# Attention scores issued as one phase of four row strips, long TensorE operations in pieces, and a new order of all queues

## The chip, the cores and the metric

The program runs on one core of a Trainium2 chip. The metric is the time of one execution in microseconds (us) of device time; lower is better. Several executions are timed and their median is given. One more execution is recorded by the hardware profiler; its page and its trace are what is quoted here. The core has five engines, each with a queue of its own that it works off in order: TensorE (PE in the profile, with the loads of its weights as PEld), ScalarE (ACT), VectorE (DVE), GpSimd (POOL) and SyncE (SP), which here only issues transfers. TensorE writes its results to PSUM, which has eight banks of 512 fp32 values in each of 128 partitions.

## The reference

Two kinds of layer alternate, A, B, A, B, on x of 2048 tokens by 512 features, with 32 heads of 16 features each. Cut to what matters:

```python
x = x + A(layernorm(x)); x = x + B(layernorm(x)); x = x + A(layernorm(x)); x = x + B(layernorm(x))

def A(x):                       # 4 segments of 512 tokens, one after the other
    q, k, v = x @ wq, x @ wk, x @ wv
    for s in range(4):
        p = softmax(qs @ ks.T * 0.25 + causal_mask)
        a_dot = p @ vs
        a_mem = (phi(qs) @ M) / (phi(qs) @ z + 1e-6)
        o_s = g * a_mem + (1 - g) * a_dot
        M += phi(ks).T @ vs; z += phi(ks).sum()
    return o @ wo

def B(x):                       # linear attention over all 2048 tokens
    q, k, v = split(x @ wqkv)
    phi(t) = concat(softmax(t @ w_phi), softmax(-(t @ w_phi)))
    kv, z = phi(k).T @ v, phi(k).sum()
    return ((phi(q) @ kv) / (phi(q) @ z + 1e-6)) @ wo
```

Here `phi` of A is `where(t > 0, t + 1, exp(t))`, and `g` is a gate for each head. Input and output are bfloat16.

## The kernel before

`Kernel.build` (line 1363) first only describes the work. Each call of `pe`, `act`, `dve`, `pool`, `either`, `copy` or `dma` makes one operation (`Program.add`, line 305), which has a number, an engine or a choice of engines, and what it reads and writes. An operation of TensorE is a list of matmuls, and it gives one signal when its last matmul is done. Nothing is issued in the order in which it is described. Four tables at the head of the file, made beforehand, settle that: `ORDER` lists the operations' numbers in one order from which every engine's queue follows; `ENGINE` has a letter for each operation that has a choice of engines (a, d, p, s for ScalarE, VectorE, GpSimd, SyncE), in the order in which these operations are made; `SLOTS` gives the buffer that each tile gets, in the order in which tiles are first used; and `AFTER` has pairs (x, y) in which operation x also waits for y. `Program.replay` (line 353) reads the tables, and `finalize` (line 411) derives the semaphore waits from reads, writes and the buffers' former holders, and writes the queues. A negative number in `ORDER` is an idle operation: so many matmuls of 240 columns on zeros (line 1431) whose result nobody reads.

For each of the two A layers and each of its four segments, `a_proj` (line 890) makes queries, keys and values of four tiles of 128 tokens. `a_att` (line 1034) makes the attention. Its work is cut into 18 units for a segment by `stages` (line 1013), 144 in all. A unit fills four PSUM banks, that is two bank pairs of 128 x 1024 scores. A head has only 16 features, so keys are laid out such that four heads stand in four strips of 32 partitions each; a score matmul uses one strip (32 rows of the array) and writes one bank. Strips 0 and 1 write the first pair, strips 2 and 3 the second. Each pair is then read by one exponential on ScalarE (line 1104) into a tile `PT`; on the diagonal, masks follow on VectorE or GpSimd (lines 1110 and 1113); and the p·v matmuls of 17 columns (16 features and the sum) multiply `PT` with `VT`. A bank pair (tile kind `st`) is (0, 1), (2, 3) or (4, 5); banks 4 to 7 also serve all other TensorE results (kinds `gen` and `pv`).

Before the change the loop at line 1078 makes two score operations for a unit, one for each bank pair, each followed by its exponential and masks. If two halves stand next to each other in `ORDER`, the second is written with 10000 added. Then `replay` makes it the first one's `mate`, joins their waits, and `finalize` issues the matmuls of the two in turn, two by two. There are 67 such pairs; the other 77 units are issued as two halves at two places of the queue.

The layers B are made by `b_keys` (line 1190: exponentials `Ek`, sums `Zk`, scaled values `Vt`, then the sum kv over tiles), `b_queries` (line 1265: exponentials of the queries, their sums `bq.sum` and the factor `rho`) and `b_out` (line 1317). B's keys and queries of a segment are worked on during the following attention. `a_out` and `b_last` project the result (`WA_o`, `WB_o`) and add it to `X` by `close` (line 1173), by VectorE or by one more matmul with the identity. `steps` (line 864) cuts a list of matmuls into operations of n matmuls; the projections use it already.

## Time and profile before

| what | us |
|---|---|
| median of 3 runs | 478.32 |
| lowest and highest | 478.20, 478.62 |
| span of the profiled execution, first to last instruction | 476.9 |
| TensorE busy | 465.2 |
| ScalarE busy | 429.7 |
| VectorE busy | 424.0 |
| GpSimd busy | 268.9 |

The profile gives the profiled execution by its span alone; the median of the runs is 1.4 us above it. The costliest groups of instructions show the attention: the exponentials, the masks, the p·v matmuls and the scores (line 520 is the helper that issues every matmul). Columns: line, engine, operation, output and inputs, count; busy us and mean ns of one; idle us of the engine before them, and what ended it.

```profile
L1104 ACT ACTIVATE PT<-PS 128x1024 bf16<-128x1024 f32 x288 | 284.6, 1083 | 7.8 <-PE PS L520 7.5
L1113 POOL TENSOR_SCALAR_AFFINE_SELECT PT<-PT 128x512 bf16<-128x512 bf16 x128 | 83.9, 664 | 30.8 <-DVE D L1110 27.4
L520 PE MATMUL PS<-VT,PT 128*128 128x17 bf16 x2048 | 82.4, 171 | 0.7 <-POOL PT L1113 0.2
L520 PE MATMUL PS<-QT,K 32*128 32x64 bf16 (+2 forms) x2176 | 77.9, 213 | 0.3
```

A group's busy time counts overlapping instructions once, and the ends of matmuls are modelled. How long a TensorE operation really holds the engine is therefore read from the start of its first matmul to the start of the next operation's first one.

### The profile page before, as it was taken

To read this page: it belongs to the slowest core of one execution; us is meant where nothing else is said; L and a number is where in the kernel's file an instruction comes from. 1 tells how busy PE (TensorE), PEld (TensorE's weight loads), DVE (VectorE), ACT (ScalarE), POOL (GpSimd) and SP (SyncE) were. 2 spreads that over 40 slices of the span, in tenths; PEclk is the share of its full clock that TensorE was granted. 3 is DMA by queue.
4 is the path that set the end of the run, shared out by engine and by line. 5 is a ranking of instruction groups with operands and counts; after the bars stand their busy time and mean duration, and the time that the engine had idled before them with its cause. 6 is when DMAs were issued, how large, how long until landed. Compare 5 with 4: busy or idle time off the path is not lost.

```text
span 476.9 us, 19206 instructions
## 1 busy us (share of the span) xinstructions
PE 465.2 (98%) x8309; PEld 319.3 (67%) x8309; DVE 424.0 (89%) x1008; ACT 429.7 (90%) x666; POOL 268.9 (56%) x435
## 2 busy tenths in 40 slices
PE   7999999999999999999999999999999999999997
PEld 6786677567756567557687666766765666665763
DVE  6999899989998988688999999999998888978885
ACT  3989999999999999986799899989999999999742
POOL 3686758656756685510267575784677578761100
DMA  8679661342422132320346417155434121313366
GB/s 264 115 202 147 144 92 25 69 69 47 48 46 47 25 65 51 36 55 4 67 62 97 74 21 134 25 75 83 59 63 63 25 47 33 51 38 58 70 128 186
DMA packets 115091, 35.86 MB, mean 75 GB/s; under 512 B 106816, under 2 KB 115008, under 8 KB 115008
## 3 DMA queue, kind: packets, MB, share of 16 engines
q1 hardware_dynamic: 112608, 32.54, 38.3%
q10 hardware_dynamic: 2400, 2.11, 1.4%
q8 instruction: 65, 1.06, 0.9%
q14 instruction: 18, 0.15, 0.1%
HBM read 6.32 MB, written 2.10 MB: 18 GB/s over the span
## 4 chain that ended last, share of the span: by engine, by line
PE 59%; DVE 18%; ACT 17%; DMA 3%; POOL 2%; issue 1%; POOLq 0%; DVEq 0%
PE PS L520 57%; ACT PT L1104 12%; DVE D L1110 2%; DVE stats L801 2%; DVE Vt L1228 2%; ACT Ek L1200 2%; DVE xn L817 1%; PE PS L601 1%; DMA EQ<-xn 1%; PE PS L1431 1%; DMA OT<-O 1%; DVE O L1139 1%; ACT K L1285 1%; DVE X L1165 1%; DVE Zk L1209 1%
## 5 line engine op out<-in xcount | busy, mean ns | idle before, releaser
L1104 ACT ACTIVATE PT<-PS 128x1024 bf16<-128x1024 f32 x288 | 284.6, 1083 | 7.8 <-PE PS L520 7.5
L1110 POOL TENSOR_TENSOR D<-PT,modd 128x256 bf16<-128x256 bf16 x133 | 91.6, 699 | 54.2 <-ACT PT L1104 39.1
L1113 POOL TENSOR_SCALAR_AFFINE_SELECT PT<-PT 128x512 bf16<-128x512 bf16 x128 | 83.9, 664 | 30.8 <-DVE D L1110 27.4
L520 PEld LDWEIGHTS PS<-VT,PT 128*128 128x128 bf16 x2048 | 75.0, 96 | 19.2 <-POOL PT L1113 2.5
L520 PE MATMUL PS<-VT,PT 128*128 128x17 bf16 x2048 | 82.4, 171 | 0.7 <-POOL PT L1113 0.2
L520 PE MATMUL PS<-QT,K 32*128 32x64 bf16 (+2 forms) x2176 | 77.9, 213 | 0.3
L520 PE MATMUL PS<-VT,D 128*128 128x17 bf16 x512 | 59.9, 170 | 0.0
L520 PEld LDWEIGHTS PS<-QT,K 32*128 32x128 bf16 x2176 | 41.5, 93 | 20.6 <-ACT PT L1104 10.5
L1110 DVE TENSOR_TENSOR D<-PT,modd 128x256 bf16<-128x256 bf16 x123 | 42.9, 362 | 2.9 <-ACT PT L1104 1.5
L520 PEld LDWEIGHTS PS<-VT,D 128*128 128x128 bf16 x512 | 43.2, 96 | 0.0
L1228 DVE TENSOR_TENSOR Vt<-PS,Zk 128x1024 bf16<-128x1024 f32 (+1 forms) x34 | 39.0, 1158 | 2.0 <-PE PS L520 1.0
L801 DVE BATCH_NORM_STATS2 stats<-X 128x6 f32<-128x512 bf16 x56 | 37.3, 681 | 2.5 <-DMA X<-in_A_x_dram 2.2
L1200 ACT ACTIVATE Ek<-PS 128x512 bf16<-128x512 f32 x64 | 37.6, 664 | 0.9 <-PE PS L520 0.9
L520 PE MATMUL PS<-WA_v,xA 128*128 128x256 bf16 x256 | 36.6, 273 | 0.1
L520 PE MATMUL PS<-WA_k,xA 128*128 128x256 bf16 x256 | 36.3, 273 | 0.2 <-POOL xA L907 0.2
L520 PE MATMUL PS<-xA,WA_q 128*128 128x128 bf16 x512 | 35.7, 219 | 0.5 <-DVE MS L986 0.2
L1165 DVE TENSOR_TENSOR X<-X,PS 128x512 bf16<-128x512 bf16 x50 | 33.7, 679 | 2.2 <-PE PS L520 1.8
L1207 POOL TENSOR_TENSOR Vt<-Ek 128x512 f32<-128x512 bf16 x24 | 27.9, 1164 | 12.9 <-ACT Ek L1200 10.4
L520 PEld LDWEIGHTS PS<-xA,WA_q 128*128 128x128 bf16 x512 | 29.8, 98 | 4.6 <-issue 0.6
L520 PE MATMUL PS<-WA_o,OT 128*128 128x512 bf16 x128 | 32.0, 380 | 0.6 <-DMA OT<-O 0.4
L520 PE MATMUL PS<-WB_o,OT 128*128 128x512 bf16 x128 | 32.1, 379 | 0.1
L1304 POOL COPY O<-rho 128x512 bf16<-128x512 bf16 x24 | 14.9, 634 | 26.5 <-DVE rho L1297 23.3
(157 smaller groups left out, 980.7 us busy)
## 6 DMA issues: line engine op xcount, KB each, us to landing
X<-in_A_x_dram SPq DMA_DIRECT2D x3, 512.0 KB, 9.9
EQ<-in_B_wqkv_dram SPq DMA_DIRECT2D x2, 512.0 KB, 5.4
out_dram<-X SPq DMA_DIRECT2D x8, 128.0 KB, 2.0
out_dram<-X ACTq DMA_DIRECT2D x8, 128.0 KB, 1.9
OT<-O SPq DMA_TRANSPOSE x42, 3.2
WB_v<-in_B_wqkv_dram SPq DMA_DIRECT2D x1, 512.0 KB, 4.3
WA_o<-in_A_wo_dram SPq DMA_DIRECT2D x1, 512.0 KB, 6.5
WB_o<-in_B_wo_dram SPq DMA_DIRECT2D x1, 512.0 KB, 4.7
```

What stands on the lines that cost most here:

```text
L520: return e.matmul(o, l, r, start=st, stop=sp, tile_position=(basep(l), basep(o)))
L601: ins = e.transpose(self.bank(gen).bitcast(BF16)[:, dt * 128:(dt + 1) * 128], src()[:, dt * 128:(dt + 1) * 128], self.ident[:])
L801: self.dve(lambda e, t=t, src=src: e.bn_stats(self.stats[:, t, :], src()), 0.603, [held() if held else R("X", t)], [R("stats", t)], name=" ...
L817: self.dve(lambda e, t=t, n=n, xn=xn: e.tensor_scalar(xn.ap[:, n], self.X[:, t, :], self.mv[:, t, 0:1], self.rstd[:, t:t + 1], op0=ALU.sub ...
L1104: self.act(lambda e, st=st, pt=pt: e.activation(pt.ap[:].rearrange("p b c -> p (b c)"), self.ps[:, st.slot[0] * 512:st.slot[0] * 512 + 102 ...
L1110: self.either(lambda e, d=d, k=k, pt=pt: e.tensor_tensor(d.ap[:, :, k, :].rearrange("p b (z c) -> p b z c", z=2), self.ends(pt.ap[:, :, 25 ...
L1113: self.pool(lambda e, q=quarters: e.affine_select(q(), q(), [[0, 4], [1, 128]], ALU.is_ge, 0.0, base=0, channel_multiplier=-1), 0.6, [pt() ...
L1165: self.dve(lambda e: e.tensor_tensor(X[:, t, :], X[:, t, :], self.bank(gen), ALU.add), 0.6, [R("X", t), gen()], [R("X", t)], name="resid")
L1200: self.act(lambda e, sgn=sgn, Ek=Ek, gen=gen: e.activation(Ek.ap[:, sgn, :], self.bank(gen), ACT.Exp, scale=1.0 - 2.0 * sgn), 512, [gen()] ...
L1207: self.pool(lambda e, Ek=Ek, sums=sums: e.tensor_tensor(sums(), *(Ek.ap[:].rearrange("p s (h j) -> p s h j", h=H)[:, :, :, 8 * k:8 * k + 8 ...
L1228: self.dve(lambda e, w=w, n=n, Vt=Vt, Zk=Zk, gen2=gen2: e.tensor_tensor(self.signed(Vt)[:, w, :, 0:16], self.bank(gen2).rearrange("p (h d) ...
L1304: P.add(("act", "pool"), {"act": lambda e, dst=dst, src=src: e.activation(dst(), src(), ACT.Copy), "pool": lambda e, dst=dst, src=src: e.t ...
```

## The change

A unit's scores become one operation. It writes both bank pairs, for each item the four strips in turn, and waits until both pairs and both `PT` tiles are free; the two exponentials and the masks follow it as before. The joining of halves (`mate`) goes away. Five kinds of TensorE operation are cut by `steps` or by hand: `state` (12 matmuls into 3 operations), `kv` and `kva` (by 4), the output projections `aout` and `bout` (by 2) and `bq.sum` (32 into 2 x 16). That takes away 144 operations and adds 138. The tables are made anew: `ORDER` has 12 idle operations with 44 matmuls where it had 33 with 129, `AFTER` has 194 pairs where it had 126, and `ENGINE` and `SLOTS` differ throughout. The matmuls of the computation themselves are the same.

```diff
-    0, 20, 26, 1, 81, 21, 24, 2, 3, 25, 27, 4, 5, 28, 22, 6, 7, 8, 9, 10, 11, 53, 18, 54, 17, 55, 60, 56, 57, 33, 61, -401, 62, 82, 63, 58, 29, 64,
...
-            op = ops[x % 10000]
+            op = ops[x]
...
-            if x >= 10000:
-                last.mate = op
-                last.need.update(op.need)
-            last = op
...
-                    if op is beside:
-                        continue
-                    beside = op.mate
-                    if beside is None:
-                        ins = op.emit[e](eng)
-                        ins.then_inc(obj(op.sem), 16 if op.isdma else 1)
-                        continue
-                    lag = max(0, len(op.mms) - len(beside.mms))
-                    for k in range(0, lag + len(beside.mms), 2):
-                        for o, k0 in ((op, k), (beside, k - lag)):
-                            for f in o.mms[max(0, k0):max(0, k0 + 2)]:
-                                ins = matmul(eng, f)
-                                if f is o.mms[-1]:
-                                    ins.then_inc(obj(o.sem), 1)
+                    ins = op.emit[e](eng)
+                    ins.then_inc(obj(op.sem), 16 if op.isdma else 1)
...
-            self.pe(mms, [PhiK(tt) for tt in range(4)] + [VT(tt) for tt in range(4)] + [R("vtone")], [gen()], name="state")
+            self.steps(mms, [PhiK(tt) for tt in range(4)] + [VT(tt) for tt in range(4)] + [R("vtone")], gen, n=4, name="state")
...
-            for y, pt in enumerate(pts):
+            P.pri = at(ts, n)
+            sts = [self.PS.tile("st") for _ in range(2)]
+            mms, reads = [], []
+
+            def put(left, item, q, c, m, sts=sts):
+                qt = QT[q // 256]
+                for a in range(4):
+                    def f(a=a):
+                        x = sts[a // 2].slot[a % 2] * 512 + c * 64
+                        return (self.ps[:, x:x + m], left(a), qt.ap[32 * a:32 * a + 32, item[1], q % 256:q % 256 + m], True, True)
+                    mms.append((f, m // 4))
...
+            self.pe(mms, reads, [st() for st in sts], pre=pts, cost=BOTH, rows=1, name="score")
+            for y, (st, pt) in enumerate(zip(sts, pts)):
                 P.pri = at(ts, n + 0.5 * y)
-                st = self.PS.tile("st")
-                mms, reads = [], []
-
-                def put(left, item, q, c, m, y=y, st=st):
-                    qt = QT[q // 256]
-                    for b in range(2):
-                        def f(a=2 * y + b, b=b):
-                            x = st.slot[b] * 512 + c * 64
-                            return (self.ps[:, x:x + m], left(a), qt.ap[32 * a:32 * a + 32, item[1], q % 256:q % 256 + m], True, True)
-                        mms.append((f, m // 4))
...
-                op = self.pe(mms, reads, [st()], pre=[pt], lat=0.23, cost=0.23, rows=y + 1, name="score")
-                op.place = (self.L, s, n)
...
         if not added:
-            self.pe(mms, reads, [gen()], name=name)
+            self.steps(mms, reads, gen, name=name)
...
-        self.pe(mms, reads + [R("ident"), R("X", t)], [gen()], name=name)
+        self.steps(mms, reads + [R("ident"), R("X", t)], gen, name=name)
...
-        self.pe([(lambda t=t, g=g, sgn=sgn: (self.bank(gen)[:, sgn * 128 + t * 32 + 8 * g:sgn * 128 + t * 32 + 8 * g + 8],
+        mms = [(lambda t=t, g=g, sgn=sgn: (self.bank(gen)[:, sgn * 128 + t * 32 + 8 * g:sgn * 128 + t * 32 + 8 * g + 8],
...
+        for k in range(0, 32, 16):
+            self.pe(mms[k:k + 16], [part(sgn, g) for sgn in range(2) for g in range(NG)] + [R("H8b")], [gen()], pre=[] if k else [rp, rho], cost=0.405, name="bq.sum")
```

The two calls that make `kv` and `kva` change from `self.pe(..., [gen()], ...)` to `self.steps(..., gen, n=4, ...)` in the same way.

74 lines of the change are left out of this document (36 added, 38 removed), and 302 rows, old and new, of tables (AFTER, ORDER).

## The prediction

> **What bounds the kernel now.** I read the page's first part, then the same sums cut into stages, then the waits, then single stretches of the timeline.
>
> ```profile
> span 476.9 us, 19206 instructions
> PE 465.2 (98%) x8309; PEld 319.3 (67%) x8309; DVE 424.0 (89%) x1008; ACT 429.7 (90%) x666; POOL 268.9 (56%) x435
> ```
>
> Read alone, this says TensorE. But three engines stand near 90%, so I cut the span at the first and the last exponential of the scores in each layer (L1104 begins at 13.0 and 238.9, ends at 202.5 and 430.5). Columns: stretch, length, busy time (and count) of each engine.
>
> ```profile
> 0.00:13.00 13.00, 10.41 (x119) 8.51 (x120) 8.57 (x28) 5.84 (x11) 4.05 (x18) 1.00 0.85 273
> 13.00:202.50 189.50, 185.67 (x3663) 128.19 (x3662) 172.53 (x429) 185.15 (x254) 125.59 (x200) 1.00 0.43 75
> 202.50:238.90 36.40, 35.93 (x411) 24.07 (x410) 32.07 (x69) 27.33 (x74) 5.86 (x12) 1.00 0.21 41
> 238.90:430.50 191.60, 190.27 (x3704) 131.22 (x3703) 176.41 (x425) 184.53 (x254) 130.19 (x203) 1.00 0.38 60
> 430.50:476.90 46.40, 42.90 (x424) 27.33 (x420) 34.43 (x62) 26.81 (x81) 3.23 (x5) 1.00 0.47 108
> ```
>
> The order is PE, weight loads, DVE, ACT, POOL. In the two attention stages, 381 of 477 us, TensorE (98 and 99%) and ScalarE (98 and 96%) are full together. So what TensorE saves there is worth only what ScalarE can follow. Between the layers and in the tail ScalarE has room and TensorE sets the pace.
>
> ```profile
> ACT PT L1104 <- PE PS L520: 7.5, 17, 1.1
> ...
> PEld PS L520 <- ACT PT L1104: 22.0, 68, 0.6
> ```
>
> The two wait for each other: TensorE 68 times for a bank pair that an exponential holds (22.0 us), ScalarE 17 times for scores (7.5 us).
>
> **The change part by part.**
>
> *Scores in one phase.* The first two rows are a unit whose halves were issued together (8 matmuls), the last two a lone half (4).
>
> ```profile
> 150.29 0.40 PE L520 MATMUL PS<-QT,K 32*128 32x256 bf16 x8
> 150.62 0.60 PE L520 MATMUL PS<-WB_k,xB 128*128 128x512 bf16 x2
> ...
> 152.37 0.39 PE L520 MATMUL PS<-QT,K 32*128 32x256 bf16 x4
> 152.69 0.60 PE L520 MATMUL PS<-WB_k,xB 128*128 128x512 bf16 x2
> ```
>
> To the next operation it is 0.33 us for the whole unit and 0.32 for half of one: two strips take as long as four. The old ORDER marks 67 of the 144 units as pairs, so 77 are issued as halves: 77 x (2 x 0.32 - 0.33) = 23.9 us less. Going into such a phase costs too:
>
> ```profile
> 108.84 0.17 PE L520 MATMUL PS<-VT,D 128*128 128x17 bf16 x1
> 108.94 0.40 PE L520 MATMUL PS<-QT,K 32*128 32x128 bf16 x16
> 109.28 0.38 PE L520 MATMUL PS<-VT,PT 128*128 128x17 bf16 x9
> 109.51 0.17 PE L520 MATMUL PS<-VT,D 128*128 128x17 bf16 x1
> ```
>
> From the last p·v matmul to the scores it is 0.10, between two p·v matmuls (109.51 - 109.28) / 9 = 0.026. Stays in this mode fall from 183 to 144 by the two ORDERs: 39 x 0.07 = 2.9. TensorE saves about 26.8 us, nearly all of it in the attention stages.
>
> *ScalarE's load.* ENGINE, read against the order in which the operations are made, leaves ScalarE 36 of the copies of q, k and v out of PSUM where it had 55; the 19 go to VectorE. A few smaller operations move too, and the new ORDER puts six Ek exponentials behind the last scores. Counted along the queues, ScalarE issues between first and last exponential 228 operations instead of 252 (layer 0) and 238 instead of 251 (layer 1).
>
> ```profile
> 13.01 3.79 ACT L1104 ACTIVATE PT<-PS 128x1024 bf16<-128x1024 f32 x4
> 16.63 0.66 ACT L579 ACTIVATE ktok<-PS 128x512 bf16<-128x512 f32 x1
> 17.10 2.01 ACT L1104 ACTIVATE PT<-PS 128x1024 bf16<-128x1024 f32 x2
> ```
>
> A copy holds ScalarE 0.47 before the next may start (16.63 to 17.10), an exponential 0.905 ((16.63 - 13.01) / 4). Of the 24, 17 are of copy size (8.3 with 0.49 for a mean) and 7 small at 0.2 to 0.3 (1.9): -10.2. Of the 13, 10 of copy size (4.9) and 3 small (0.7): -5.6. With ScalarE's idle time as it is (4.4 and 7.1 us), the stages shorten by these 15.8 us; TensorE's 26.8 is enough to allow it.
>
> *Both pairs at once.* The added wait: a unit's scores now wait until two bank pairs are free, and TensorE, in order, holds everything behind them: p·v, projections, and through these VectorE. SLOTS gives 41 of 288 tiles the third pair; at 89 of the 143 steps from unit to unit the new scores overwrite the pair that the exponential just before must release.
>
> ```profile
> 183.08 1.96 ACT L1104 ACTIVATE PT<-PS 128x1024 bf16<-128x1024 f32 x2
> ...
> 185.56 1.02 ACT L1104 ACTIVATE PT<-PS 128x1024 bf16<-128x1024 f32 x1 [0.52 <-PE PS L520]
> ```
>
> That is the round trip, end of an exponential to start of the next through TensorE: 0.52 us. All 89 have other ScalarE work queued in between: 30 one operation (about 0.49), the rest two or more. The cover just holds if TensorE comes to the scores in time; it can be late by one piece, 2 x 0.216 = 0.43 (next rows). At the 30, from 0 to 0.2 each (half a piece): 0 to 6 us; I take +2, nearer to the covered case, since all waits of this kind are 7.5 us now.
>
> *Pieces.* 138 new boundaries.
>
> ```profile
> 205.71 1.03 PE L520 MATMUL PS<-WA_o,OT 128*128 128x512 bf16 x4
> ...
> 216.98 1.89 PE L520 MATMUL PS<-xB,WB_q 128*128 128x512 bf16 x8
> ```
>
> Four unsplit matmuls step at (1.03 - 0.38) / 3 = 0.217; eight of a projection already issued in twos at (1.89 - 0.38) / 7 = 0.216: a boundary is free. By ORDER 91 of the 138 run on at once; 47 let something in. There the sum is done, and its bank free, up to a score phase (0.33) later; what waits is a residual on VectorE, at most 47 x 0.33 = 15 us off the path, and I take 0. AFTER's waits (126 to 194) are all of GpSimd for VectorE; behind each stand masks, for which p·v waits. I cost them at nothing, GpSimd being 56% busy; without that cover they delay p·v, not the scores. The transposing DMAs of SP's queue are sorted anew with their producers; none is added.
>
> *Start.* The old ORDER opens with 25 matmuls on zeros, the new one has 4.
>
> ```profile
> 1.04 3.58 PE L1431 MATMUL PS<-warm 128*128 128x240 bf16 x17 [1.04 <-DVE warm L702]
> ```
>
> ```profile
> 1.04 4.43 PE L1431 MATMUL PS<-warm 128*128 128x240 bf16 x25 [1.04 <-DVE warm L702]
> ...
> 7.75 1.06 PE L520 MATMUL PS<-WA_k,xA 128*128 128x256 bf16 x8
> 8.64 1.95 PE L520 MATMUL PS<-xA,WA_k 128*128 128x128 bf16 x32
> ```
>
> Seventeen take 3.58 (0.21 each), the last eight 0.85 more (0.106): for its first 3.4 us TensorE runs at half speed, though the column of the granted clock says 1.00. Now the real matmuls pay that: half of 3.4 = +1.7. Against it, the 8 key matmuls (7.75 to 8.64) move behind the first score: -0.9. Together +0.8, bounds 0 (VectorE is the later one there) to 3.4. The Trainium skill, "TensorE: Matmul & The Clock Gate", Part 1, says the window is free-running and has to be a busy one, so the slow time depends on its phase; by it the term could be 3.4 instead of 1.7 (an estimate), and the sum 1.7 higher. The 3.4 us of slow matmuls agree with it; the phase no row shows.
>
> *Between the layers and tail.* Operations leave the attention stages and land here: between the layers net 64 short matmuls (p·v and sums, 0.026), 24 of 136 columns (0.06, below), four of 512 (0.216), eight of 128 and 256 (0.08): 1.7 + 1.4 + 0.9 + 0.6 = 4.6, less 17 zero matmuls at 0.106 (1.8): +2.8. Tail: 32 p·v, eight of 512, four of 128: +2.8, less 14 zero matmuls: +1.4. ScalarE's and VectorE's share lies under TensorE here.
>
> ```profile
> 464.59 0.64 PE L520 MATMUL PS<-Rkv,EQ 128*128 128x136 bf16 x8
> ...
> 465.06 1.03 PE L520 MATMUL PS<-WB_o,OT 128*128 128x512 bf16 x4
> ```
>
> Eight of 136 columns take 0.47, 0.06 each. Three output stores go from ScalarE's queue to SP's; both have gaps there: nothing.
>
> **Sum**: +0.8 - 10.2 + 2.8 - 5.6 + 1.4 + 2 = -8.8; 476.9 - 8.8 = 468.1. The median of the runs, 478.32, lies 1.4 above the profiled span, which I take as what lies around it: **469.5 us**.
>
> **The rivals.**
>
> *TensorE's gain passes whole* (13%). ScalarE's idle time in the attention stages, 189.5 - 185.2 + 191.6 - 184.5 = 11.4 us, goes as well, since TensorE is never late: 469.5 - 11.4 = 458. For it: the 98% of the page. Against it: ScalarE would be at 100% over 350 us. The Trainium skill, "TensorEngine Tiling (Array Packing)", PSUM Bottleneck, says that after tiling the PSUM copy may become the bottleneck; by it this case falls away.
>
> *VectorE becomes the bound* (13%).
>
> ```profile
> L579 DVE CAST QT<-PS 128x512 bf16<-128x512 f32 x12 | 8.2, 683 | 0.4 <-PE PS L520 0.2
> L1110 DVE TENSOR_TENSOR D<-PT,modd 128x256 bf16<-128x256 bf16 x123 | 42.9, 362 | 2.9 <-ACT PT L1104 1.5 <-PE PS L520 1.1
> L801 DVE BATCH_NORM_STATS2 stats<-X 128x6 f32<-128x512 bf16 x56 | 37.3, 681 | 2.5 <-DMA X<-in_A_x_dram 2.2
> ```
>
> It gets 19 copies at 0.68 and 10 masks at 0.36, 16.5 us, of which, counted along the queues with what leaves, some 5 stay in each attention stage. The fullest long stretch it has now:
>
> ```profile
> 25.00:95.00 70.00, 67.54 (x1320) 48.68 (x1320) 66.82 (x170) 67.67 (x93) 50.09 (x82) 1.00 0.61 114
> ```
>
> 66.82 / 70 = 95.5%. If that is its limit, the stages need (172.5 + 5) / 0.955 = 185.9 and (176.4 + 5) / 0.955 = 189.9, 5.3 shorter in all; with the other terms (+7.0, or +5 without the coupling) it ends at 478 to 480. Against it: packed operations overlap,
>
> ```profile
> 7.67 1.28 DVE L801 BATCH_NORM_STATS2 stats<-X 128x6 f32<-128x512 bf16 x2
> ```
>
> two in 1.28, where one has 0.68, so a fuller queue takes fewer busy us and 95% is not yet its end.
>
> *The pairs couple TensorE and ScalarE* (18%, slower). At the 89 steps, ScalarE's covering work itself waits for matmuls queued behind the blocked scores, and part of the 0.52 comes bare. It decides from 10.8 / 89 = 0.12 us each (10.8 is the sum without the +2). With 0.22, less than half a round trip, it costs 19.6: 478.3 + 8.8 = 487. For it: with halves one pair filled while the other drained, and 77 units used that. The Trainium skill, "TensorEngine Tiling (Array Packing)", Gotcha 1: PSUM Pressure, says that row tiles write to different banks and that software must see to the order; by it a phase of four strips holds more banks at once, and the chance of this case rises. No run here shows it yet. Against it: the cover counted above.
>
> **How the numbers follow.** Forecast 56% (464 to 475), TensorE whole 13% (455 to 463), VectorE 13% (476 to 481, of which 3 points lie below 477.3, 6 within 0.2% and 4 above), coupling 18% (480 to 495). A measurement here tells 0.2%, about 1 us, from no change. Faster: 56 + 13 + 3 = 72%; same 6%; slower 18 + 4 = 22%. Leaving out the ends of the outer cases, the range is 459 to 485.
>
> **What would show it.** Right: no score group of 4 or 14 matmuls ends a stay in the timeline; ScalarE near 419 us busy and still 96% or more in the attention stages, which last about 179 and 186; the wait of weight loads for L1104 not above 22. Start: the first matmuls after the transposes step at twice the 0.109. VectorE's case: its share over 97% and ScalarE's below 94. Coupling: L1104 waits for TensorE over 20 us. What would make me wrong most likely is the cover at the pair change.

## The result, and the profile after

The changed kernel takes **476.06 us** (median of 20 runs, 472.86 to 480.45), the kernel before 478.36 (20 runs, 477.63 to 479.26). The ratio is 0.9947, with a 95% interval of 0.9929 to 0.9964: 0.5% faster. The ratios compare the means of the executions, without those that lie over 1.5% above the fastest of their kernel. The forecast was 469.5. The direction and the range held, but of the 8.8 us forecast only 2.3 came. The profiled execution of after took 476.89 (span 474.9). Its lines stand twelve earlier than in before: L508 issues the matmuls, L1092 is the exponential, L1153 the residual on VectorE. In the rows of the experiments on after they are L519, L1103 and L1164.

The page's first part, after:

```profile
span 474.9 us, 18936 instructions
PE 430.7 (91%) x8157; PEld 301.6 (64%) x8224; DVE 418.5 (88%) x1036; ACT 420.8 (89%) x644; POOL 260.3 (55%) x429
```

The work went as forecast. ScalarE lost 8.9 us of busy time (429.7 to 420.8, forecast "near 419"). TensorE lost 34.5 by this page (465.2 to 430.7), but that is too much: 67 of its matmuls, all of 512 columns, are missing in this profile (8157 matmuls for 8224 weight loads). The experiments below that have the same matmuls and complete records show 436 to 439 us, so it lost 26 to 29. Yet no engine is full any more. Where the time stayed is seen in the same five stages (length, busy time of PE, weight loads, DVE, ACT, POOL, then the granted clock, the busy share of the DMA engines and GB/s):

```profile
0.00:12.90 12.90, 7.03 (x97) 6.63 (x98) 8.05 (x25) 4.76 (x8) 4.63 (x19) 1.00 0.79 253
12.90:198.40 185.50, 167.39 (x3578) 118.53 (x3602) 168.24 (x444) 176.15 (x230) 119.01 (x194) 0.99 0.44 75
198.40:238.90 40.50, 38.36 (x437) 26.12 (x443) 34.31 (x70) 31.88 (x84) 6.70 (x13) 0.96 0.26 50
238.90:426.30 187.40, 174.72 (x3639) 123.44 (x3669) 171.38 (x437) 180.13 (x239) 124.71 (x194) 1.00 0.41 60
426.30:474.90 48.60, 43.23 (x415) 26.91 (x418) 36.55 (x64) 27.88 (x86) 5.26 (x10) 0.99 0.51 109
```

| stage | before | after | moved by | forecast |
|---|---|---|---|---|
| start | 13.0 | 12.9 | -0.1 | +0.8 |
| attention, layer 0 | 189.5 | 185.5 | -4.0 | -10.2 |
| between the layers | 36.4 | 40.5 | +4.1 | +2.8 |
| attention, layer 1 | 191.6 | 187.4 | -4.2 | -5.6 |
| tail | 46.4 | 48.6 | +2.2 | +1.4 |

In the attention stages (forecast together -15.8, or -13.8 with the coupling; measured -8.2) ScalarE's busy time fell by 13.4 (185.15 + 184.53 less 176.15 + 180.13), but its idle time rose from 11.4 to 16.6 (372.9 less 356.3), where the forecast kept it. TensorE, idle for 5 us there before, is idle for 30.8 by the page (21 to 27 in four experiments with nearly the same order whose records are complete). So both engines now wait. ScalarE's idle time did not rise everywhere: it went from 4.4 to 9.4 in layer 0 and from 7.1 to 7.3 in layer 1. Of the 6.8 us by which the profiled span misses the forecast (474.9 against 468.1), layer 0's attention alone has 6.2; the other stages and the coupling term nearly cancel. The waits of after name for what (first column: who waits, for whom; us in all, times, longest):

```profile
PEld PS L508 <- ACT PT L1092: 25.4, 64, 1.1
...
ACT PT L1092 <- PE PS L508: 10.9, 17, 2.7
...
DVE X L1153 <- PE PS L508: 7.9, 12, 1.4
PE PS L508 <- DMA OT<-O: 7.8, 8, 1.5
```

The last row is nearly new (before it was 0.4 us, once): TensorE waits for transposing transfers. `OT` is A's output `O`, transposed by a DMA of SP's queue, and the weights of the output projection. Before and after by the groups of the page (before first):

```profile
L520 PE MATMUL PS<-WA_o,OT 128*128 128x512 bf16 x128 | 32.0, 380 | 0.6 <-DMA OT<-O 0.4
```

```profile
L508 PE MATMUL PS<-WA_o,OT 128*128 128x512 bf16 x114 | 31.1, 385 | 10.2 <-DMA OT<-O 6.3
```

The idle time ahead of A's output projections went from 0.6 to 10.2 us. Some 3 us of that are the 14 missing matmuls (128 - 114, at 0.217); in two experiments with complete records and the same order on TensorE it is 6.3 and 6.8. One such place in the timeline of after shows who inherits it (start, length, engine, operation, in brackets the idle time before it and what ended that):

```profile
181.33 0.81 PE L508 MATMUL PS<-WA_o,OT 128*128 128x512 bf16 x3 [1.18 <-DMA OT<-O]
...
182.18 0.69 DVE L1153 TENSOR_TENSOR X<-X,PS 128x512 bf16<-128x512 bf16 x1 [1.35 <-PE PS L508]
...
182.54 1.02 ACT L1092 ACTIVATE PT<-PS 128x1024 bf16<-128x1024 f32 x1 [0.85 <-PE PS L508]
```

TensorE waits about 1 us for the transfer (1.18 in the row, which lacks the first of the four matmuls); behind the projection stand the scores, so the residual on VectorE comes 1.35 and the next exponential 0.85 late. All three engines lose the same microsecond. In layer 0 four such exponentials, at 91.85, 117.53, 161.53 and 182.54, wait 5.6 us behind four such projections; all waits of layer 0's exponentials for scores rose from 2.4 to 7.6 us. The chain of the work that ended last agrees; its shares by engine, before and then after:

```profile
PE 59%; DVE 18%; ACT 17%; DMA 3%; POOL 2%; issue 1%; POOLq 0%; DVEq 0%
```

```profile
PE 38%; DVE 27%; DMA 14%; ACT 14%; POOL 3%; issue 3%; SPq 0%; DVEq 0%; POOLq 0%
```

TensorE's part fell by 21 points, and transfers and VectorE took 20 of them. Why are the transfers late? Two stretches of after's transfers, each with one such transpose in it (queue, packets, MB, share of the 16 engines; below, the issue with its time to landing):

```profile
q1 hardware_dynamic: 1056, 0.26, 37.8%
issues: line engine op xcount, KB each, median us to landing
OT<-O SPq DMA_TRANSPOSE x1, 3.1
```

```profile
q1 hardware_dynamic: 1056, 0.26, 26.8%
q8 instruction: 1, 0.02, 1.2%
q14 instruction: 1, 0.01, 0.5%
issues: line engine op xcount, KB each, median us to landing
OT<-O SPq DMA_TRANSPOSE x1, 4.8
```

The second met a 16 KB piece of TensorE's own program (queue q8, 65 such pieces in the run). Of all 100 transposing transfers, those during which no piece of program moved (q8 or q14) took 3.03 to 3.42 us (39 in before, with one more at 3.79; 35 in after); where a piece of q8 began 1.0 to 3.0 us behind the issue, 21 of 30 in before and 28 of 31 in after took 4.0 or more. Of the 14 wide transposes in the attention stages 12 landed within 3.3 us in before (the others took 3.9 and 4.9); in after, 7 took 4.46 to 5.07, each with a piece that began 2.0 to 2.9 us behind the issue. TensorE was done with the matmul ahead of their first use 4.2 to 5.5 us behind the issue in before (median 4.6) and 2.8 to 4.9 in after (median 4.0); two of them it reached even before a landing within 3.3 us. So the new order leaves them less room than the old, and more of them meet a piece and land late. This is the reading that the experiments are to try.

### The profile page after: what moved, and what is told of

Its sections match the earlier page's. It is cut to its first block, busy times and chain, and to the rows that moved or that the text cites. A ratio compares the mean times of both kernels' runs of the same rounds, so it can differ in the third digit from the quotient of the medians.

```text
span 474.9 us, 18936 instructions
## 1 busy us (share of the span) xinstructions
PE 430.7 (91%) x8157; PEld 301.6 (64%) x8224; DVE 418.5 (88%) x1036; ACT 420.8 (89%) x644; POOL 260.3 (55%) x429
## 3 DMA queue, kind: packets, MB, share of 16 engines
q10 hardware_dynamic: 1968, 1.71, 1.1%
## 4 chain that ended last, share of the span: by engine, by line
PE 38%; DVE 27%; DMA 14%; ACT 14%; POOL 3%; issue 3%; SPq 0%; DVEq 0%; POOLq 0%
PE PS L508 37%; ACT PT L1092 10%; DMA OT<-O 7%; DMA xA<-xn 3%; DVE Vt L1216 3%; DVE stats L789 2%; DVE xn L805 2%; DVE O L1127 2%; DVE D L1098 1%; DMA OT<-EQ 1%; DMA xB<-xn 1%; DVE QT L567 1%; PE PS L589 1%; DMA EQ<-xn 1%; POOL D L1098 1%
## 5 line engine op out<-in xcount | busy, mean ns | idle before, releaser
L1092 ACT ACTIVATE PT<-PS 128x1024 bf16<-128x1024 f32 x288 | 278.9, 1054 | 11.8 <-PE PS L508 10.9
L1098 POOL TENSOR_TENSOR D<-PT,modd 128x256 bf16<-128x256 bf16 x123 | 81.4, 673 | 56.6 <-DVE D L1098 16.1
L1101 POOL TENSOR_SCALAR_AFFINE_SELECT PT<-PT 128x512 bf16<-128x512 bf16 x128 | 80.4, 639 | 38.0 <-DVE D L1098 19.2
L508 PEld LDWEIGHTS PS<-VT,PT 128*128 128x128 bf16 x2048 | 75.0, 96 | 19.8 <-issue 3.3
L508 PE MATMUL PS<-VT,PT 128*128 128x17 bf16 x2048 | 81.1, 171 | 2.5 <-POOL PT L1101 0.8
L508 PE MATMUL PS<-VT,D 128*128 128x17 bf16 x512 | 60.1, 171 | 0.0
L508 PE MATMUL PS<-QT,K 32*128 32x64 bf16 (+2 forms) x2176 | 56.2, 213 | 2.3 <-ACT PT L1092 1.0
L508 PEld LDWEIGHTS PS<-VT,D 128*128 128x128 bf16 x512 | 43.2, 96 | 0.0
L1153 DVE TENSOR_TENSOR X<-X,PS 128x512 bf16<-128x512 bf16 x50 | 33.6, 679 | 8.4 <-PE PS L508 7.9
L508 PEld LDWEIGHTS PS<-QT,K 32*128 32x128 bf16 x2176 | 29.4, 93 | 18.2 <-ACT PT L1092 11.1
L508 PE MATMUL PS<-WA_o,OT 128*128 128x512 bf16 x114 | 31.1, 385 | 10.2 <-DMA OT<-O 6.3
L1098 DVE TENSOR_TENSOR D<-PT,modd 128x256 bf16<-128x256 bf16 x133 | 38.4, 311 | 2.1 <-PE PS L508 1.4
L508 PE MATMUL PS<-xA,WA_q 128*128 128x128 bf16 x512 | 36.2, 219 | 1.5 <-DMA xA<-xn 1.0
L1293 POOL COPY O<-rho 128x512 bf16<-128x512 bf16 x27 | 16.5, 633 | 38.3 <-DVE EQ L1301 10.8
L508 PE MATMUL PS<-WA_k,xA 128*128 128x256 bf16 x256 | 35.9, 273 | 0.3 <-DVE MS L976 0.3
L508 PE MATMUL PS<-WA_v,xA 128*128 128x256 bf16 x256 | 34.8, 273 | 0.7 <-DVE QT L567 0.2
L508 PEld LDWEIGHTS PS<-xA,WA_q 128*128 128x128 bf16 x512 | 30.1, 98 | 5.8 <-issue 1.3
L508 PE MATMUL PS<-WB_o,OT 128*128 128x512 bf16 x117 | 30.5, 379 | 0.8 <-issue 0.2
## 6 DMA issues: line engine op xcount, KB each, us to landing
WB_o<-in_B_wo_dram SPq DMA_DIRECT2D x1, 512.0 KB, 10.2
```

What stands on the lines that cost most here:

```text
L508: return e.matmul(o, l, r, start=st, stop=sp, tile_position=(basep(l), basep(o)))
L1092: self.act(lambda e, st=st, pt=pt: e.activation(pt.ap[:].rearrange("p b c -> p (b c)"), self.ps[:, st.slot[0] * 512:st.slot[0] * 512 + 102 ...
L1098: self.either(lambda e, d=d, k=k, pt=pt: e.tensor_tensor(d.ap[:, :, k, :].rearrange("p b (z c) -> p b z c", z=2), self.ends(pt.ap[:, :, 25 ...
L1101: self.pool(lambda e, q=quarters: e.affine_select(q(), q(), [[0, 4], [1, 128]], ALU.is_ge, 0.0, base=0, channel_multiplier=-1), 0.6, [pt() ...
L1153: self.dve(lambda e: e.tensor_tensor(X[:, t, :], X[:, t, :], self.bank(gen), ALU.add), 0.6, [R("X", t), gen()], [R("X", t)], name="resid")
L1293: P.add(("act", "pool"), {"act": lambda e, dst=dst, src=src: e.activation(dst(), src(), ACT.Copy), "pool": lambda e, dst=dst, src=src: e.t ...
```

## The experiments

Each was run beside the kernel before; the ratio is to that kernel, with its 95% interval (after: 0.9947, 0.9929 to 0.9964). Time is the median.

**Which engine bounds.** Four kernels load or relieve one engine alone. Scores in two phases of two strips, at the same places:

```diff
+            mms = [f for k in (0, 2) for i, f in enumerate(mms) if i % 4 in (k, k + 1)]
```

> The kernel after with the phase alone undone: each unit's matmuls are issued strips 0 and 1 first, then strips 2 and 3, in the same operation at the same place. That is two phases of 0.31 instead of one of 0.33, 144 x 0.29 = 42 us more of TensorE. If TensorE's time is what the change won, and the new order has only some slack, 495 to 512 (TensorE at 98 to 99% again, and more waits). If TensorE's time is covered by the waits that the profile shows (44 us idle of 475), 478 to 485. The ratio of the difference to 42 us is what a microsecond of TensorE is worth now.

Measured: 478.91, ratio 0.9994 (0.9974 to 1.0014). This undid less than was expected: from a unit's scores to the next operation it is 0.445 us instead of 0.342 for the 64 units of 28 matmuls, 0.355 instead of 0.335 for the 32 of 16 and 0.337 instead of 0.330 for the 48 of 8 (medians), not 0.29 more each, as two phases apart would cost. Side by side the two phases take little more than one. That puts 6.6 + 0.6 + 0.3 = 7.5 us on TensorE, not 42, and 2.9 us came out (2.2 by the ratios): some 0.3 to 0.4 for each.

Exponentials of 960 instead of 1024 columns, on after and on before:

```diff
+                w = 1024 if (self.L, s) == (0, 0) else 960
...
-                    pt.ap[:].rearrange("p b c -> p (b c)"), self.ps[:, st.slot[0] * 512:st.slot[0] * 512 + 1024], ACT.Exp, scale=0.25), 1024, [st()], [pt()], name="exp")
+                    pt.ap[:].rearrange("p b c -> p (b c)")[:, 0:w], self.ps[:, st.slot[0] * 512:st.slot[0] * 512 + w], ACT.Exp, scale=0.25), 1024, [st()], [pt()], name="exp")
```

> The kernel after with 252 of the 288 exponentials over 960 of 1024 columns (all but those of the first segment of the first layer; the last 64 columns of the second bank keep what was in the buffer). That takes 252 x 53 ns = 13.4 us from ScalarE and nothing from the others. If ScalarE is what bounds the attention stages, as predicted, 462.5 to 465. If waits for TensorE and the transfers bound them, ScalarE only gets more idle: 470 to 475.

> The kernel before, with the same 252 exponentials over 960 columns as e8: 13.4 us less of ScalarE. The prediction let ScalarE's load pass to the time one to one in the attention stages, because ScalarE was busy for 97% of them. If that was so before the change already, 465 to 468. If TensorE held it up there (98% busy, 59% of the chain), 476 to 478.5.

Measured on after: 476.17, ratio 0.9939 (0.9918 to 0.996), though ScalarE has 13.4 us less work (252 exponentials, 0.903 us from one start to the next with 1024 columns and 0.850 with 960), 10.8 in busy time by the page (420.8 in after):

```profile
PE 431.6 (91%) x8157; PEld 303.3 (64%) x8224; DVE 416.5 (88%) x1036; ACT 410.0 (86%) x644; POOL 260.8 (55%) x429
```

On before: 475.87, ratio 0.9934 (0.9919 to 0.995), 3.0 us for the same 13.4: 0.22. So ScalarE did not set the pace one for one **even before the change**, where it was 96 to 98% busy. And VectorE, with 117 masks on half their width:

```diff
+                            w = 1 if e is self.nc.vector and full else 2
```

> The kernel after with 117 of VectorE's 133 odd masks (all but those of the first segment of the first layer) over one bank of the pair instead of both (128 of 256 columns; the other half of D keeps what was in the buffer). That takes about 117 x 0.13 = 15 us from VectorE and nothing from the others. If VectorE has become the bound (rival of the prediction), 461 to 465. If no engine alone bounds the attention stages, as e7 and e8 let expect (0.15 to 0.2 us for each us taken, at full clock), 472 to 475.

Measured: 473.63, ratio 0.9912 (0.988 to 0.9945); 9.1 us less VectorE work (418.5 to 409.4) gave 2.4, though this interval still meets after's. On after, the shorter exponentials gave nothing at the median; their executions had a lower clock (0.982 to 0.992), and reckoned to full clock, as below, they stand at 471.0 against after's 472.6, which is 1.6 for 13.4. So a microsecond of an engine is worth between nothing and some 0.4 here. These prices lie near the engine's share in the chain of work: ScalarE in before 0.22 (share 17%), in after 0 to 0.12 (14%), VectorE in after 0.27 (27%), TensorE in after 0.3 to 0.4 (38%). Each rests on a difference of 3 us or less, so the nearness is no more than a hint.

**Does the wait for the transfers cost it?** A first try moved the pieces of the program against the work: 112 waits that are long met at the head of TensorE's queue of after, and in before 73 matmuls of 82 columns on zeros in place of 25 of 240.

```diff
+                if e == "pe":
+                    for _ in range(112):
+                        eng.wait_ge(obj(("e", "dve")), 1)
```

```diff
+        n, w = (73, 41) if n == 25 else (n, 120)
```

> The kernel after, with 112 waits that are already met put at the head of TensorE's queue, where it waits for the first data anyway: every later 16 KB piece of TensorE's program now begins 56 matmuls earlier in the work. Nothing else changes. Theory 'code pieces': in the profile of the kernel after, 8 of the 14 transposing transfers that feed the out projection take 4.5 to 5.1 us instead of 3.2, and each of them has a 16 KB transfer of TensorE's program in its packets; TensorE stands before these projections for 10.6 us in all. By the positions of the pieces 4 of the 14 are met after the shift: the median of OT<-O falls from 4.5 to about 3.3 us, TensorE's wait for OT<-O in the attention from 7.8 to 3 to 5 us, and the time from 476.1 to 473 to 475. Theory 'clock' (stretches of half rate after gaps of TensorE): 476.1 within 0.7 us. Theory 'coupling' (both bank pairs needed at once): 476.1 within 0.7 us.

> The kernel before, with its 25 opening matmuls on zeros of 240 columns issued as 73 of 82 columns: the same columns, but the pieces of TensorE's program begin 48 matmuls earlier in the work. By their positions 7 of the 14 transposing transfers of the out projection meet a piece, where 2 did. Theory 'code pieces': the median of OT<-O rises from 3.2 to about 4.5 us, the out projection begins to wait, and the time rises from 478.4 to 480 to 482. By the other theories nothing changes: 478.4 within 0.5.

Measured: 479.98, ratio 0.9999 (0.9975 to 1.0024), and 479.99, ratio 1.0025 (1.0009 to 1.004). The first was a miss: the waits lengthened the start to 15.2 us, and 8 of the 14 transfers still came late. In before 5 came late instead of 2, and it was 0.25% slower. Neither settles anything on after.

Next the wait itself was taken away: A's output projections read `WA["q"]` as their weights instead of `OT`, in after and in before. That frees them not of the transfer alone, but of all that goes before it, the attention's output and its normalisation too.

```diff
-        mms = [(lambda g=g, gen=gen: (self.bank(gen), oT.ap[:, c, g, :], self.WA["o"][:, g, :], g == 0, g == 3 and not added), 512) for g in range(NG)]
-        self.close(t, gen, mms, [oT(), R("WA", "o")], added, True, "aout")
+        mms = [(lambda g=g, gen=gen: (self.bank(gen), self.WA["q"][:, g, 0:128], self.WA["o"][:, g, :], g == 0, g == 3 and not added), 512) for g in range(NG)]
+        self.close(t, gen, mms, [R("WA", "q"), R("WA", "o")], added, True, "aout")
```

> The kernel after, with the out projections of A multiplying weights that lie in place since the start instead of OT, so that they no longer wait for the transposing transfer (which is still issued; the output of A is not computed). All else is the same, also the sizes. Theory 'queue' (TensorE stands before these projections for 10.6 us in all, ScalarE and VectorE behind it, and the clock falls after it): 469 to 472, the granted clock mostly 0.995 or more. If the waits would only come up elsewhere: 475 to 477.

> The kernel before with the edit of e10: the out projections of A multiply weights that lie in place instead of OT and wait for no transposing transfer (the output of A is not computed). In the profile of the kernel before TensorE stands before these projections for 0.6 us where it is 10.6 us after. If the wait is new with the change, 476.5 to 478.5 (a gain of 0 to 2, against 9 in e10). If it was there all along and only hidden in the profile, 469 to 472.

On after: **467.13**, ratio 0.9757 (0.9736 to 0.9778), 8.9 us below after. On before: 478.89, ratio 0.9999 (0.999 to 1.0007), nothing. The attention stages of both, the one on after first:

```profile
13.40:193.10 179.70, 168.94 (x3606) 118.25 (x3603) 168.27 (x444) 175.28 (x230) 118.30 (x194) 1.00 0.45 76
...
233.60:418.60 185.00, 177.61 (x3668) 123.65 (x3667) 170.37 (x437) 179.32 (x239) 124.59 (x194) 1.00 0.41 61
```

```profile
12.80:203.20 190.40, 185.42 (x3664) 128.24 (x3665) 172.37 (x429) 185.56 (x254) 125.23 (x200) 1.00 0.42 75
...
239.30:431.00 191.70, 190.28 (x3703) 131.09 (x3702) 176.54 (x425) 184.54 (x254) 129.87 (x203) 1.00 0.38 60
```

Without the wait the stages are 179.7 and 185.0 long, where the forecast had "about 179 and 186", and ScalarE's idle time in them is back at 10.1 (364.7 less 354.6), below before's 11.4. ScalarE's share of the chain rises as well:

```profile
PE 34%; ACT 32%; DVE 21%; DMA 9%; issue 1%; POOL 1%; SPq 0%; DVEq 0%; POOLq 0%
```

So waiting for `OT` is worth nothing in the old order and 8.9 us in the new: that contrast is shown, and layer 0's exponentials wait 2.7 us for scores there instead of 7.6. How far it carries is limited by the last two runs below.

**A better order?** Scores and what they need earlier on TensorE (twelve moves), then VectorE's queue with it (thirteen), then sixteen more of both with 25 opening zeros, then these with 30 zeros in six waits. One move of the first and one of the second, as they stand in `ORDER` (985 is work of TensorE, 806 of VectorE):

```diff
-    963, 724, 985, 920, 722,
+    963, 724, 920, 722,
...
-    719, 945, 720, 721,
+    719, 945, 985, 720, 721,
```

```diff
-    965, 803, 806, 827, 974,
+    965, 803, 827, 974,
...
-    976, 973, 725, 978,
+    976, 973, 806, 725, 978,
```

> The kernel after, with 12 changes of TensorE's order: where an operation that waits for a transposing transfer stands in front of scores, p.v or sums that are ready sooner, these go first. Theory 'queue' (TensorE works off its queue in order and is blocked by these operations, and ScalarE runs dry behind it): ScalarE's idle time in the attention stages falls from 16.6 to 10 to 12 us, and the time from 476.1 to 471.5 to 474. Theory 'coupling': the scores wait for both pairs wherever they stand, 476.1 within 0.7. Theory 'clock': a small gain of up to 1 us, as some gaps go.

> The kernel after with the 12 changes of TensorE's order of e3 and 13 of VectorE's: where VectorE waits over 0.35 us for a projection, a transfer or a reciprocal, ready masks, sums, copies and scalings go first. All is computed. Theory 'both queues' (the late transfer stops TensorE at the projection and VectorE at the residual behind it): 470 to 473.5. Theory 'chain' (the row normalisation, transfer, projection, residual, layernorm is late itself, whatever goes ahead of it): 475 to 477.

> e14_both_queues with 16 more operations of TensorE and VectorE moved ahead of waits of over 0.4 us that its own trace shows, and the 25 opening zeros of the kernel before. If what is left of the forecast gain is in such waits, 470.5 to 473; if the waits only change their place by now, 473 to 475.

> e15 with 30 zeros in six waits of TensorE of 0.6 to 2 us (40 to 60% of each). If stretches of half rate cost about 1.5 us each, as the executions of all these kernels show, and are avoided, 1 to 2 us less than e15 and a granted clock of 0.996 or more; otherwise the same.

| order | time | ratio | interval |
|---|---|---|---|
| TensorE's 12 moves | 476.83 | 0.9932 | 0.9904 to 0.996 |
| and VectorE's 13 | 473.81 | 0.9897 | 0.9876 to 0.9918 |
| and 16 more | 483.16 | 1.008 | 1.0055 to 1.0106 |
| and 30 zeros | 476.32 | 0.9954 | 0.993 to 0.9977 |

The first took TensorE's idle time ahead of the projections from 10.2 us (some 7 without the missing records) to 3.4 and gained nothing that can be told from after: ScalarE's idle time in the attention stages stayed (17.7). The second beats after, but its interval meets the first one's, and its waits moved rather than went (rows as in after's table of waits above, where the same two are 7.9 and 7.8):

```profile
DVE X L1164 <- PE PS L519: 9.9, 13, 2.2
...
PE PS L519 <- DMA OT<-O: 3.0, 3, 1.4
```

The third, by the same reasoning, was 7 us *slower* than after: a plain miss. The span and clock of its profile, and below them those of the fourth order, say where to look (over all twelve executions the clock is 0.975 to 0.996 in the third and 0.986 to 0.996 in the fourth):

```profile
core 0: 485.6 us, clock 0.979
```

```profile
core 0: 473.2 us, clock 0.996
```

The fourth is the third with 30 matmuls on zeros that nobody reads, and it takes 6.8 us less. By the price of the clock below, some 3 of these go with the clock; the rest is not explained.

**The clock.** In before the granted clock is 0.999 or 1.000 in all but 4 of 123 executions; in after 18 of 20 lie below 1.000. The lost share comes in stretches of 3.41 us (or twice that) at half rate; after's profile has them at 115.7 and 201.05. At the first (timeline of after):

```profile
114.57 0.81 PE L508 MATMUL PS<-WA_o,OT 128*128 128x512 bf16 x3 [2.26 <-DVE r L991]
...
115.37 1.56 PE L508 MATMUL PS<-WA_o,OT 128*128 128x512 bf16 x4
...
117.53 1.02 ACT L1092 ACTIVATE PT<-PS 128x1024 bf16<-128x1024 f32 x1 [2.73 <-PE PS L508]
```

Three matmuls take 0.81 behind an idle gap; the next four of the same form take 1.56, the last of them at a step of 0.43 where 0.217 was seen, and an exponential gets its scores 2.73 us late. The gap itself is one of the late transfers: the `OT` of these matmuls was issued at 109.22, met a piece of program and landed at 114.22, 0.1 us before the first weight load (a copy of VectorE, `KV`, ended at the same time, and the first matmul's record is missing, so the row names another). So at this place the two causes can't be told apart. To try the clock alone, zeros were put into TensorE's waits: 98 in nine waits; 233 in 39; 238 and 25 opening ones into the twelve moves; 44 in seven waits and 25 opening ones on top of the first 98.

```diff
-    333, 209, 350, 171,
+    333, 209, -150, 350, 171,
...
-    1481, 1471, 1516, 1472,
+    1481, 1471, -213, 1516, 1472,
```

(-150 stands for 9 matmuls in bank 5, -213 for 13 in bank 4.)

> The kernel after, with 98 matmuls on zeros put into nine of the waits of TensorE of over 1 us (9 to 16 each, in front of the operation that waits), so that it does not stand still there. Theory 'clock': the granted clock is 1.00 in nearly all executions, the spread of the times falls from 7.6 us (472.9 to 480.5) to about 2, and the median to about 473. Theories 'code pieces' and 'queue': the waits stay and so does the time, 476 to 477, apart from what the pieces do that come up to 98 matmuls earlier towards the end.

> The kernel after, with 233 matmuls on zeros in 39 places: in front of every operation for which TensorE stood still over 0.3 us in the profile, as many as fit the wait, in a bank that is free then. Theory 'clock': in each run so far a stretch of half rate (3.41 us or twice that) follows a stretch of 3.41 us in which matmuls were busy for less than 62%; with the waits filled none is that low, so the granted clock is 0.998 or more in nearly all executions, the spread falls from 7.6 us to 3 or less and the median from 476.1 to 472.5 to 474. Theory 'queue' (TensorE's blocked queue alone makes ScalarE run dry, the clock costs nothing): 475.5 to 477.

> The kernel of e3_scores_first, with its own waits of over 0.3 us filled in the same way (238 matmuls on zeros in 42 places) and 25 matmuls on zeros at the start, as the kernel before has them. Theory 'clock': as e5_fill, 472 to 474. Theories 'clock' and 'queue' together: both gains, 469.5 to 472. Neither: 475 to 477.

> A version that may beat both: e4_zero_fill with 44 more zeros in seven of its own waits that no exponential ends (60% of each wait), and the 25 opening zeros of the kernel before. If the waits for transfers are filled without delaying anything, the granted clock is 0.996 or more and the time 471.5 to 474; if zeros delay what they stand before, as 233 of them did (e5), 476 to 480.

| zeros | time | ratio | interval |
|---|---|---|---|
| 98 | 475.16 | 0.9904 | 0.988 to 0.9928 |
| 233 | 483.96 | 1.0096 | 1.0072 to 1.0121 |
| 238 + 25, twelve moves | 481.75 | 1.0044 | 1.002 to 1.0069 |
| 98 + 44 + 25 | 474.41 | 0.9907 | 0.9893 to 0.9922 |

Few zeros in long waits gain 1 to 2 us (the first interval lies just clear of after's, the last one further). The 233 keep the clock at 0.999 to 1.0 and still lose 7.9, the 238 lose 5.7 (clock 0.989 to 1.0): a zero stands in order before real work and delays it. Over the executions of all these kernels, each with a level of its own and one slope, 1% of clock goes with 4.1 us (standard error 0.6), about 1.5 us for a stretch. At full clock after would by that stand at 472.6 and the kernel without the transfer wait at 465.9: of after's distance of 6.5 us to the forecast, some 3.5 goes with the clock. This slope is a correlation over executions, not a run that gives the clock back alone; what brings a stretch on is counted in the last section.

**Short zeros at the start alone.** Last, after with nothing changed but 96 matmuls of 56 columns (or 112 of 48) on zeros ahead of everything. This warms TensorE for the first real matmuls and moves every later piece of its program by as many matmuls.

```diff
 ORDER = (
+    -1537,
     21, 24, 25, 0,
...
+            w = 28 if n == 96 else 120
...
-                ins = e.matmul(self.ps[:, b * 512 + 272:b * 512 + 512], self.warm[:], self.warm[:, None, 0:120].to_broadcast([128, 2, 120]), start=True, stop=True)
+                ins = e.matmul(self.ps[:, b * 512 + 272:b * 512 + 272 + 2 * w], self.warm[:], self.warm[:, None, 0:w].to_broadcast([128, 2, w]), start=True, stop=True)
```

> The kernel after with 96 matmuls on zeros of 56 columns at the very start, where TensorE waits for data. By the positions of the program's pieces in the trace of the kernel after, 9 of the 14 transposing transfers of the out projection would meet one (8 without the shift). Theory 'code pieces': slower than e18 by 2 to 4 us. Otherwise within 1 us of e18.

> The same with 112 matmuls of 48 columns: nearly the same columns (5376 each), and the pieces 16 matmuls earlier than in e17. By the positions 3 of the 14 transfers would meet one. Theory 'code pieces': 2 to 4 us faster than e17, 472 to 474, fewer transfers over 4 us. Otherwise within 1 us of e17.

Measured: **468.43**, ratio 0.9778 (0.9755 to 0.9801), and 469.82, ratio 0.9786 (0.9754 to 0.9819). Nothing of the computation is left out in them, and they beat both kernels: 6 to 8 us below after, 9 to 10 below before. The stages of the first:

```profile
0.00:12.60 12.60, 9.58 (x193) 8.84 (x194) 8.06 (x25) 4.80 (x8) 4.64 (x19) 1.00 0.79 243
12.60:195.70 183.10, 168.53 (x3578) 120.37 (x3604) 167.95 (x444) 175.45 (x230) 118.38 (x194) 0.98 0.46 78
195.70:233.30 37.60, 37.19 (x438) 25.43 (x442) 34.27 (x70) 31.88 (x86) 6.76 (x13) 1.00 0.35 53
233.30:418.10 184.80, 173.81 (x3645) 123.54 (x3673) 170.34 (x437) 179.42 (x239) 124.92 (x194) 1.00 0.39 61
418.10:466.30 48.20, 43.30 (x411) 26.70 (x412) 36.50 (x64) 27.89 (x86) 5.26 (x10) 1.00 0.51 110
```

The gain lies in the three middle stages (2.4, 2.9 and 2.6 us), hardly at the start. Between the layers the clock is 1.00 instead of 0.96; that stage lost a stretch at half rate. But the first attention stage has two (0.98), where after's has one, and over their executions the clock is 0.992 to 0.995 with 96 zeros and 0.989 to 1.000 with 112, where after has 0.985 to 1.000. So more clock is not what these zeros bring. ScalarE's idle time in attention falls from 16.6 to 13.0. But the contrast that was expected between the two missed: 5 and 6 of the 14 transfers were late, not 9 and 3, and their times do not differ. And the second one's waits for `OT` are nearly as long as after's (7.8 and 10.2 there, with the same number of records missing):

```profile
PE PS L519 <- DMA OT<-O: 6.6, 5, 2.4
...
L519 PE MATMUL PS<-WA_o,OT 128*128 128x512 bf16 x114 | 32.1, 395 | 9.9 <-DMA OT<-O 5.7
```

So the length of that wait alone does not give the time. **What stays open**: which of the things that these zeros shift (where the pieces of the program fall, when each operation runs, which places the slow stretches of the clock hit) brings the 7 us. 112 waits at the same place did not bring it, and 25 zeros of 240 columns were tried only together with other changes.

## Why the prediction came out as it did

**ScalarE's load, -15.8: nearly right in its load, wrong in its price.** Busy time fell by 13.4 of the 15.8 counted. "With ScalarE's idle time as it is (4.4 and 7.1 us), the stages shorten by these 15.8 us" is the step that failed: idle time became 9.4 and 7.3, and the stages shortened by 8.2. It failed in layer 0 (4.0 instead of 10.2), where the exponentials wait 5.6 us behind four late transfers; in layer 1 it nearly held (4.2 instead of 5.6). The premise below it, that two engines full together make ScalarE the pace, fails already in before, where 13.4 us less of its work gave 3.0. The chain of work had said so: ScalarE held 17% of it in before, with 98 and 96% busy time in these stages.

**Pieces at nothing: the term that was left out.** "The transposing DMAs of SP's queue are sorted anew with their producers; none is added" was costed at nothing without a look at how much room each had until its first use. Their number stayed, their room and their landing did not: the room fell from a median of 4.6 us to 4.0, 7 of 14 took 4.46 to 5.07 us where 2 had taken 3.9 and 4.9, and taking away the wait for them gives 8.9 us in after and none in before; with it gone the stages are as forecast. Since a shift of the same order by zeros comes within a microsecond of the forecast too (468.4 and 469.8 against 469.5), it isn't the order in itself that costs the missing 6.5 us, but what its waits meet in time; the transfers are one such meeting that is shown, and the rest of the split is open, since 112 zeros leave the wait for the transfers as long and still take 6 us off. The direction, too, is in part luck: with its start alone shifted the same order ran from 468.4 to 480.0 us, against 478.4 for before.

**The cover at the pair change, +2**, named as what would most likely be wrong: it held in the main. L1092 waits 10.9 us for TensorE where L1104 waited 7.5, far from the 20 that the coupling rival needed, and single long waits (2.73 at the clock, 0.85 behind a transfer) are not a 0.22 at each of 89 steps. Three marks of a right forecast failed: the wait of weight loads for the exponential is 25.4, where it was to be "not above 22"; ScalarE is busy for 95% of layer 0's attention, not 96; and the attention stages last 185.5 and 187.4, not 179 and 186. Two-strip phases side by side in the new order were slower than after, not faster.

**VectorE's bound**: its case was given 476 to 481, and 476.06 lies at the edge of that, but for another reason. Its share in the attention stages is 91% (168.24 / 185.5 and 171.38 / 187.4), not over 97.

**TensorE's 26.8**: right (26 to 29 less busy time). Its price is what the two phases show: 7.5 us more of TensorE cost 2 to 3.

**Start, +0.8**: the slow step came (32 key matmuls held TensorE 2.94 us, from 7.50 to 10.44, where before they took 1.79), and lay hidden: the first scores began at 12.32 instead of 12.55.

**Between the layers, +2.8, and tail, +1.4**: 4.1 and 2.2. The first holds a stretch at half rate (clock 0.96); without it, in the kernel with 96 zeros, it is +1.2. Behind the start no term of the forecast had the clock, since before ran at 1.00 throughout.

## What to carry to other kernels

Where several engines are near 95% busy, a microsecond taken from one is not worth a microsecond: here it was worth between nothing and 0.4, nearer to the engine's share in the chain of work than to its busy share. Shorten that engine alone in an experiment before you count on more. When an order is made anew, list for every transfer the room between its issue and its first use, and set its slowest landing against that rather than its median: a projection behind a late transpose stops three engines at once. And when a kernel gets idle gaps that it did not have, look at the granted clock, and at how much the time moves when only zeros are added at the start, before the order itself is blamed.

## What the runs showed of the hardware

**A transposing transfer met by a piece of program lands late**: 3.03 to 3.42 us alone, 4.0 or more in 49 of the 61 cases in which one began 1.0 to 3.0 us behind the issue. The Trainium skill, "Runtime: NRT & Kernel Launch", section "Instruction fetch mechanics", says that instructions come in blocks of 16 KiB and that crossing into the next is mostly hidden. The blocks agree (65 pieces of 16 KB on q8, about one for 128 matmuls with their weight loads); whether TensorE itself waits for one, no row tells. That another queue's transfer lands 1 us and more later with one is seen here alone, as the coincidence of these 49; no run moved a piece and nothing else.

**The clock falls without a long gap.** Of the windows of 3.41 us in the profiles up to the 30 zeros in six waits (without the start and the end of each) in which matmuls were busy for less than 45%, all 9 were followed by half rate; at 45 to 55%, 9 of 17; at 55 to 60%, 3 of 9; at 60 to 80%, 5 of 119; above, 4 of 2126. One of these four, at 200.3 in the order with twelve moves, followed a window that was full, but of short matmuls of 8, 17 and 136 columns; so the busy share of the profile is no more than a rough sign, and missing records make some windows look emptier than they were. The Trainium skill, "TensorE: Matmul & The Clock Gate", Part 1, puts the window at 3413 ns, which agrees, and gives as the rule no idle gaps of TensorE of more than about 3.4 us. After's longest single gap behind the start is 2.26 us, and it lost the clock all the same: one wait of 2.26 us in a window, and one of 1.71 in another, were enough.

**Matmuls on zeros change the time of the same order by 15 us**: with only zeros added to after's order, the medians run from 468.4 (96 at the start) to 484.0 (233 in its waits, which also delay work). With nothing but the start changed, by zeros or by waits, they run from 468.4 to 480.0. A single order's time says less about the order than that.

**Two two-strip score phases side by side** take 0.34 us (8 matmuls) to 0.44 (28), a four-strip phase 0.33 to 0.34, and before's lone two-strip phase 0.32. So half phases are dear mainly where they stand apart: two apart 0.64, two together at most 0.44.
